# Chunked attention followed by a squared-ReLU feed-forward layer on one core: block 0 worked by halves of the heads, and a new order of block 2's loads

## The chip, the cores and the metric

The kernel runs on one core of one Trainium2 chip. Its time is the device time of one launch in microseconds (us). The time before is the median of 3 runs; beside it stands one execution that the hardware profiler recorded.

## The reference: what is computed

```python
q_c, k_c, v_c = (t.reshape(B, H, nc, 64, D) for t in (q, k, v))       # B, H, S, D = 8, 8, 576, 64
attn = softmax(q_c @ k_c.transpose(0, 1, 2, 4, 3) / sqrt(D))          # each chunk of 64 tokens by itself
x    = (attn @ v_c).transpose(0, 2, 1, 3).reshape(B * S, H * D)       # 4608 tokens x 512
h    = maximum(x @ w_in, 0)                                           # w_in 512 x 2048
out  = h * h @ w_out                                                  # w_out 2048 x 512, float32
```

All inputs and the output are float32 in DRAM. The kernel computes in bfloat16 and accumulates in float32.

## The kernel before, in words

**Groups and blocks.** The 4608 tokens are 18 groups of 256 tokens (four chunks of 64); two groups are a block of 512 tokens, so there are nine blocks. For a group the kernel loads q, k and v, transposes q and k so that the head dimension lies on the partitions, multiplies chunk by chunk into scores (`scores`, matmuls in L483), takes the exponential on ScalarE (L494), and multiplies with v (`values`, L510). V has a column of ones beside each head, so the last column of a product is the sum of a row of weights; VectorE takes its reciprocal (L442) and multiplies (L443) into x. Transposed x (`xT`) goes into the feed-forward layer. Its first half (`ffn_in`, L579) computes, for each of 16 tiles `ft` of 128 features, four matmuls over `dt`, the four slices of 128 of the 512 columns of x. Heads 0 and 1 make slice 0, heads 6 and 7 make slice 3. ScalarE applies ReLU out of PSUM (L590), VectorE or ScalarE squares (L598, L596). The second half multiplies with `w_out` (`ffn_out_by_ft`, L901, in block 0; `ffn_out` with sums of sub-matrices, L780, in the later blocks; from block 4 on the first half, too, is built from sums of sub-matrices, L657).

**The order of the work.** It is written out by hand: each engine executes its instructions in the order in which the program emits them. The start (L967 to L1002) is straight code; after it each block has a table of slots, one per feature tile or group of matmuls, which says what is emitted behind which slot (`at(slot, f, ...)`, L1004 to L1077). Attention of a later block is thus laid between the feed-forward matmuls of an earlier one.

**The start before.** SP's queue gets the loads of q and k for groups 0 and 1 (all eight heads, 256 tokens each), then V in nine pieces, then `w_in` by slices of 256 columns (`load_w_in`: all 512 rows, so the first slice carries feature tiles 0 and 1), then `w_out`. q and k of each group arrive as rows of two neighbouring tokens (512 bytes for each head). TensorE transposes q0, k0, q1 (`transpose_paired`, L400), makes the scores of group 0, transposes k1, and goes on through scores, values and the transposes of x (`transpose_x_early`, L521). Between these, `keep_busy(n)` (L433) issues n matmuls of 128 columns whose results nobody reads: 8, 6, 10, 4 and 8. The first feed-forward matmul comes after the last transpose of x. Tiles 0 and 1 are done in two halves of 256 tokens, since the second half of xT is copied last. GpSimd casts the weights to bfloat16 in slices (L334, L342); ScalarE casts one half of the first slice (L333).

**Buffers.** The PSUM pool `ps_ffn` has four banks, taken in turn; two double banks `ps_att` and `ps_att2` serve attention in turn. Staged weights go through five buffers `w_st`; q and k through five buffers `qk_st`. V lies in five tiles `ve_sb` (even heads) and eleven tiles `vo_sb` (odd heads, whose chunks are shifted by 64 tokens). The loads of SP's queue share eight completion semaphores in turn, so from the ninth on a load is issued when the one eight before it has landed.

**Blocks 1 and 2.** From group 4 on, q and k are not transposed by TensorE: GpSimd casts them (`C`, L449 and L454) and SP issues a transposing DMA (`TD`, L460). While block 0 runs, SP issues the loads of block 2 (groups 4 and 5): q and k of both, then V of group 4, then V of group 5. While block 1 runs, SP issues the two transposing DMAs (slots 21 and 25), then the loads of q and k of groups 6 and 7. The scores of groups 4 and 5 come at slots 36 and 37 of block 1, their values at 38 and 40.

## Time and profile before

| | before |
|---|---|
| time, median of 3 runs | 278.54 us (277.97 to 279.36) |
| time of the profiled execution | 276.91 us |
| its span, first to last instruction | 275.1 us |
| granted TensorE clock | 1.000 |
| TensorE (PE), busy share of the span | 96% |
| VectorE (DVE) | 72% |
| ScalarE (ACT) | 61% |
| GpSimd (POOL) | 33% |

The profiled execution's own time is 1.8 us longer than its span: that much lies before its first and after its last instruction. Times within the trace count from the first instruction. A row of a timeline gives the start, the length, engine, line, operation, names (out<-in), the count, and in brackets the idle time of the engine just before with what ended it. PE's matmuls overlap, so the length of a group has the last one's way through the array in it. For SP's queue (SPq) a row is the issue of a DMA, not its transfer; its length holds what the issue had to wait for.

### The profile page before, as it was taken

The page shows a single profiled execution, that of the slowest core. Times are in us where ns is not written, and L with a number is a line of the kernel's source. Part 1 is how long each engine was busy: PE and PEld are TensorE (multiplying, and loading weights), DVE is VectorE, ACT ScalarE, POOL GpSimd, SP SyncE. Part 2 cuts the span into 40 slices and gives each one's busy share as a digit, 9 for nine tenths or more (in the row PEclk, how much of TensorE's full clock was granted, in tenths as well). Part 3 has the DMA queues.
Part 4 walks back from the last instruction along what each step waited for, and adds up shares of the span by engine and source line. Part 5 has one row for each costly group of instructions (what it writes and reads, how often), then busy time and mean ns, then how long its engine had stood idle before and what let it go on. Part 6 is the DMA issues. An engine that isn't in the chain of part 4 may idle for free.

```text
span 275.1 us, 7923 instructions
## 1 busy us (share of the span) xinstructions
PE 264.9 (96%) x3261; PEld 203.4 (74%) x3261; DVE 199.2 (72%) x365; ACT 168.3 (61%) x300; POOL 89.6 (33%) x122
## 2 busy tenths in 40 slices
PE   2999999999999999999999999999999999999995
PEld 2764445888774588447878888888888888888884
DVE  1457514999538592499989998799779877994752
ACT  1657614894458883877678765565746665756430
POOL 2048834240360012040245224551643212331600
PEclk9999999999999999999999999999999999999999
DMA  7999999999999999999999999697999530220223
GB/s 216 262 352 389 361 332 270 339 213 172 262 210 218 238 234 218 275 223 178 228 236 197 218 238 194 103 220 196 244 187 224 123 76 2 99 55 7 71 83 114
DMA packets 136056, 55.60 MB, mean 202 GB/s; under 512 B 104273, under 2 KB 131921, under 8 KB 136017
## 3 DMA queue, kind: packets, MB, share of 16 engines
q1 hardware_dynamic: 133248, 46.54, 74.0%
q0 software_dynamic: 2624, 8.39, 9.6%
q8 instruction: 26, 0.43, 0.6%
q10 hardware_dynamic: 144, 0.13, 0.1%
q14 instruction: 14, 0.11, 0.1%
HBM read 36.70 MB, written 9.44 MB: 168 GB/s over the span
## 4 chain that ended last, share of the span: by engine, by line
PE 87%; DMA 4%; SPq 3%; DVE 3%; ACT 1%; issue 1%; ACTq 0%; DVEq 0%
PE ps_ffn L657 22%; PE ps_out L780 22%; PE ps_ffn L579 17%; PE ps_ffn L780 14%; PE ps_ffn L901 5%; PE ps_att L510 3%; PE ps_att L540 2%; DMA vo_sb<-in_v_dram 2%; PE ps_att L483 2%; DMA xT<-x 2%; DVE gT L598 2%; SPq L266 1%; SPq L308 1%; SPq L312 1%; DVE x L443 1%; ACT e L494 1%
## 5 line engine op out<-in xcount | busy, mean ns | idle before, releaser
L579 PE MATMUL ps_ffn<-xT,w_in_bf 128*128 128x512 bf16 (+1 forms) x328 | 57.8, 333 | 0.0
L780 PEld LDWEIGHTS <-w_st 128*128 128x128 bf16 x512 | 48.9, 98 | 6.6 <-DVE w_st L614 0.5
L665 DVE CUSTOM_DVE_ANT_0 relu<-ps_ffn,w_st 128x512 f32<-128x512 f32 x60 | 39.3, 684 | 13.0 <-PE ps_ffn L657 11.6
L579 PEld LDWEIGHTS <-w_in_bf 128*128 128x128 bf16 x328 | 31.2, 98 | 21.6 <-POOL w_in_bf L334 0.2
L598 DVE TENSOR_TENSOR gT<-relu 128x256 bf16<-128x256 bf16 (+2 forms) x68 | 34.1, 537 | 17.8 <-ACT relu L590 17.3
L590 ACT ACTIVATE relu<-ps_ffn 128x256 bf16<-128x256 f32 (+2 forms) x82 | 39.4, 501 | 9.4 <-PE ps_ffn L579 8.6
L657 PE MATMUL ps_ffn<-qk_st,w_in_bf 128*128 128x256 bf16 x240 | 35.3, 273 | 0.1
L657 PEld LDWEIGHTS <-w_in_bf 128*128 128x128 bf16 x320 | 30.7, 98 | 4.1 <-issue 0.3
L809 POOL DMA_DIRECT2D out_dram<-o_sb x24 | 17.6, 733 | 43.6 <-DVE o_sb L614 23.3
L780 PEld LDWEIGHTS <-gT 128*128 128x128 bf16 x296 | 28.6, 98 | 3.3
L780 PE MATMUL ps_out<-w_out_bf,w_st 128*128 128x256 bf16 x240 | 30.8, 273 | 0.0
L699 ACT ACTIVATE w_st<-ps_ffn 128x512 f32<-128x512 f32 x20 | 11.9, 597 | 29.6 <-PE ps_ffn L657 29.6
L443 DVE TENSOR_TENSOR x<-ps_att,recs 128x512 bf16<-128x512 f32 x36 | 24.9, 692 | 1.2
L657 PEld LDWEIGHTS <-qk_st 128*128 128x128 bf16 x240 | 22.6, 98 | 3.2 <-DVE qk_st L614 0.3
L657 PE MATMUL ps_ffn<-xT,qk_st 128*128 128x256 bf16 x160 | 23.9, 273 | 0.0
L676 POOL TENSOR_TENSOR qk_st<-relu 128x512 bf16<-128x512 f32 x10 | 10.3, 1034 | 41.6 <-DVE relu L665 38.1
L494 ACT ACTIVATE e<-ps_att 128x1024 bf16<-128x1024 f32 x18 | 18.3, 1025 | 8.5 <-PE ps_att L483 8.5
L676 POOL TENSOR_TENSOR gT<-relu 128x512 bf16<-128x512 f32 x10 | 10.3, 1033 | 35.4 <-DVE relu L665 30.5
L449 POOL CAST qkb<-qk_st 128x1024 bf16<-128x1024 f32 x12 | 13.0, 1082 | 14.9 <-DMA qk_st<-in_q_dram 14.9
L674 ACT ACTIVATE gT<-relu 128x512 bf16<-128x512 f32 x28 | 17.7, 631 | 0.0
L780 PE MATMUL ps_ffn<-w_out_bf,w_st 128*128 128x256 bf16 x144 | 17.7, 273 | 0.0
L614 DVE TENSOR_TENSOR w_st<-gT,w_st 128x1024 bf16<-128x1024 bf16 x26 | 16.8, 682 | 0.0
(92 smaller groups left out, 428.7 us busy)
## 6 DMA issues: line engine op xcount, KB each, us to landing
qk_st<-in_q_dram SPq DMA_DIRECT2D x16, 512.0 KB, 5.6
out_dram<-o_sb POOLq DMA_DIRECT2D x28, 256.0 KB, 3.9
qk_st<-in_k_dram SPq DMA_DIRECT2D x24, 256.0 KB, 5.6
ve_sb<-in_v_dram SPq DMA_DIRECT2D x32, 128.0 KB, 3.9
w_st<-in_moe_w_in_dram SPq DMA_DIRECT2D x8, 512.0 KB, 5.9
w_st<-in_moe_w_out_dram SPq DMA_DIRECT2D x8, 512.0 KB, 5.5
vo_sb<-in_v_dram SPq DMA_DIRECT2D x24, 128.0 KB, 3.6
qk_st<-in_k_dram SPq DMA_DIRECT2D x4, 512.0 KB, 5.8
```

Source lines behind the costliest of these rows:

```text
L443: nc.vector.tensor_tensor(out=x, in0=o[:, :, :, 0:D], in1=rec.to_broadcast([128, 2, n, D]), op=ALU.mult)
L494: nc.scalar.activation(out=e_out, in_=s_in, func=AF.Exp, scale=scale)
L579: nc.tensor.matmul(out=h[:, 0:n], lhsT=w_in_bf[:, dt, ft * 128:(ft + 1) * 128], rhs=xT[:, c // 128:(c + n) // 128, dt, :], start=(dt == 0) ...
L590: nc.scalar.activation(out=rl[:, 0:n], in_=h[:, 0:n], func=AF.Relu)
L598: nc.vector.tensor_tensor(out=dst, in0=src, in1=src, op=ALU.mult)
L614: nc.vector.tensor_tensor(out=out, in0=in0, in1=in1, op=op)
L657: nc.tensor.matmul(out=bank[:, f * GT:(f + 1) * GT], lhsT=a[:, dt, ft * 128:(ft + 1) * 128], rhs=b[:, :, dt, :], start=(first and f == 0 a ...
L665: nc.vector._custom_dve(TENSOR_ADD_SAT, out=out, in0=in0, in1=in1, s0=BIG, s1=0.0)
L674: engine.activation(out=dst, in_=r, func=AF.Square)
L676: engine.tensor_tensor(out=dst, in0=r, in1=r, op=ALU.mult)
L780: nc.tensor.matmul(out=out_ps, lhsT=lhsT, rhs=b[:, i, :], start=(first and i == 0 and (last or t == 0)), stop=(i == HF - 1), skip_group_ch ...
L809: dma.dma_start(out=out[t0:t0 + GT, col:col + HD].rearrange("(t p) d -> p t d", p=128), in_=o_sb.rearrange("p (t d) -> p t d", d=HD))
```

## The change

Three things change at the start, and one in blocks 1 and 2.

**Halves.** Block 0 is split by heads, not by tokens. Half 0 is heads 0 to 3 of all 512 tokens, half 1 heads 4 to 7. q and k arrive as rows of four neighbouring tokens (1,024 bytes for each head). V of a half is six loads: for each pair of heads the even head (four tiles of 128 tokens) and the inner three tiles of the odd head, and two half tiles at the edges. A half has the same count and shapes of transposes (32), scores matmuls (32), exponentials (one of 128x1024), values matmuls (two times 16), reciprocals and multiplies as a group had. The copies of transposed k are shared: one by ScalarE, one by VectorE; those of q stay on VectorE.

**Loads.** SP's order becomes q, k, V of half 0; q, k of half 1; rows 0 to 255 of the first 512 columns of `w_in` (in two loads); V of half 1; rows 256 to 511 of the same columns (in two loads); then `w_in` from slice 2 on as before. GpSimd casts all of it; ScalarE's cast is gone.

**TensorE's order.** Since half 0 yields slices 0 and 1 of x, the feed-forward tiles 0 to 3 start before half 1 is done: their matmuls for dt 0 and 1 stand behind the scores of half 1 and around its values, those for dt 2 behind the transposes of x, then those for dt 3 with ReLU and square. The four tiles hold the four banks of `ps_ffn` meanwhile. All 64 matmuls of block 0's first half have 512 columns (before, 16 of 72 had 256). Of the `keep_busy` matmuls 16 of 36 stay: 8 before the scores of half 0 and 8 behind them. The square of tile 3 in block 0 goes to VectorE.

**Block 2.** While block 0 runs, SP gets q and k of groups 4 and 5 and V of group 4 alone. In block 1 the casts and transposing DMAs of groups 4 and 5 are emitted at slots 16 and 20, and V of group 5 at slot 21, behind both transposing DMAs.

```diff
+    v_first = w_pool.tile([128, 4, n_hp, D + 1], FP32, name="ve_first")
+    v_mid = w_pool.tile([128, 3, n_hp, D + 1], FP32, name="vo_mid")
...
-            if i == 0 and c:
-                return lambda: nc.scalar.copy(out=w_in_bf[:, :, c:c + n], in_=st[:, :, c:c + n])
...
+    def load_w_in_half(r):
+        st = w_st[next(n_staged) % 5].rearrange("p (a f) -> p a f", a=2)
+        for c in (0, 256):
+            nc.sync.dma_start(
+                out=st[:, :, c:c + 256],
+                in_=moe_w_in[256 * r:256 * r + 256, c:c + 256].rearrange("(a p) f -> p a f", p=128))
+            nc.gpsimd.tensor_copy(
+                out=w_in_bf[:, 2 * r:2 * r + 2, c:c + 256], in_=st[:, :, c:c + 256])
...
+        for hp in range(NH):
+            copy = nc.vector.tensor_copy if hp or not which else nc.scalar.copy
+            copy(out=qkT[:, which, hp].rearrange("c (p i) -> c p i", i=4),
+                 in_=psb[:, hp].rearrange("c i p -> c p i"))
...
+    def first_tile(ft, dts):
+        if dts[0] == 0:
+            first_h.append(ps_ffn.tile([128, 512], FP32, name="ps_ffn"))
+        for dt in dts:
+            nc.tensor.matmul(
+                out=first_h[ft],
+                lhsT=w_in_bf[:, dt, ft * 128:(ft + 1) * 128],
+                rhs=xTs[0][:, :, dt, :],
+                start=(dt == 0), stop=(dt == n_dt - 1), skip_group_check=True)
+
+    def first_in():
+        for ft in range(4):
+            first_tile(ft, (3,))
+            squared(0, ft, first_h[ft], 0, BT, ft)
+            yield
+        yield from ffn_in(0, [(0, BT, range(4, n_ft))])
...
+    for half in range(2):
+        qk_half, v_half = half_loads(half)
+        go(qk_half)
+        if half:
+            load_w_in_half(0)
+        go(v_half)
+    load_w_in_half(1)
+    transpose_half(0, 0, ffn_bank())
+    transpose_half(0, 1, ffn_bank())
     keep_busy(8)
...
+    scores_half(0)
     keep_busy(8)
...
+    values_half(0, 0)
+    values_half(0, 1)
+    transpose_half(1, 0, ffn_bank())
+    transpose_x_half(0, 0, ffn_bank(), act)
+    transpose_half(1, 1, ffn_bank())
+    transpose_x_half(0, 1, ffn_bank(), act)
+    scores_half(1)
+    first_tile(0, (0, 1))
+    first_tile(1, (0, 1))
+    values_half(1, 0)
+    first_tile(2, (0, 1))
+    values_half(1, 1)
+    first_tile(3, (0, 1))
+    transpose_x_half(1, 0, att_bank()[:, 0:256], act)
+    transpose_x_half(1, 1, att_bank()[:, 0:256], nc.vector.tensor_copy)
+    for ft in range(4):
+        first_tile(ft, (2,))
+    first_ffn_in = first_in()
...
-            loads, go_slots = pieces(far), range(17)
+            loads, go_slots = itertools.chain(*map(qk_pieces, far), v_pieces(far[0])), range(17)
...
-                for slot, f in ((16 + 4 * i, C), (21 + 4 * i, TD), (36 + i, SC), (38 + 2 * i, AV),
+                for slot, f in ((16 + 4 * i, C), (16 + 4 * i, TD), (36 + i, SC), (38 + 2 * i, AV),
                                 (41 + 2 * i, XT)):
                     at(slot, f, g)
+            at(21, lambda: go(v_pieces(nxt[1])))
```

More of the change, by code (lines that the diff above doesn't have):

```diff
@@ L239 @@
     n_rec = itertools.count()
-    v_even = [w_pool.tile([128, 2, n_hp, D + 1], FP32, name=f"ve_sb{i}") for i in range(NV)]
-    v_odd = [w_pool.tile([128, n_hp, D + 1], FP32, name=f"vo_sb{i}") for i in range(NO)]
+    v_first = w_pool.tile([128, 4, n_hp, D + 1], FP32, name="ve_first")
+    v_mid = w_pool.tile([128, 3, n_hp, D + 1], FP32, name="vo_mid")
+    v_even = [v_first[:, 2 * i:2 * i + 2] for i in range(2)] + [
+        w_pool.tile([128, 2, n_hp, D + 1], FP32, name=f"ve_sb{i}") for i in range(2, NV)]
+    v_odd = [v_mid[:, i - 1] if 0 < i < 4 else w_pool.tile(
+        [128, n_hp, D + 1], FP32, name=f"vo_sb{i}") for i in range(NO)]
     for vt in v_even:
@@ L314, in v_pieces @@
                 in_=v[b, 1::2, s:s + m, :].rearrange("h s d -> s h d")))
-        if g < 2:
-            yield from [even[0], *odd[:-1], even[1], odd[-1]]
-        else:
-            yield from even + odd
+        yield from even + odd
     def go(pieces):
@@ L515, in values, with half_loads, rows, even @@
             out_of_x(x[:, t].rearrange("p h a d -> p a h d"), ps, n_hp)
-    def transpose_x_early(g, t):
-        psb = ps_ffn.tile([128, 512], FP32, name="ps_ffn").bitcast(BF16)
-        x = state["x", g]
-        for hp in range(n_hp):
+    NH, HH = 2, H // 2
+    def half_loads(half):
+        b, s0 = chunks[0][0]
+        hs = slice(HH * half, HH * half + HH)
+        def rows(which, src):
+            return lambda: nc.sync.dma_start(
+                out=loaded(half, which).rearrange("p (h e) -> p h e", h=HH),
+                in_=src[b, hs, s0:s0 + BT, :].rearrange("h (s i) d -> s h (i d)", i=4))
+        hps = slice(NH * half, NH * half + NH)
+        def even(hp):
+            return lambda: nc.sync.dma_start(
+                out=v_first[:, :, NH * half + hp, 0:D],
+                in_=v[b, HH * half + 2 * hp, s0:s0 + BT, :].rearrange("(t p) d -> p t d", p=128))
+        def odd(hp):
+            return lambda: nc.sync.dma_start(
+                out=v_mid[:, :, NH * half + hp, 0:D],
+                in_=v[b, HH * half + 2 * hp + 1, s0 + CH:s0 + BT - CH, :].rearrange(
+                    "(t p) d -> p t d", p=128))
+        def edge(n):
+            p = CH if n == 0 else 0
+            s = s0 + 128 * n - CH + p
+            return lambda: nc.sync.dma_start(
+                out=v_odd[n][p:p + CH, hps, 0:D],
+                in_=v[b, HH * half + 1:HH * half + HH:2, s:s + CH, :].rearrange("h s d -> s h d"))
+        return [rows(0, q), rows(1, k)], [even(0), odd(0), edge(0), edge(4), even(1), odd(1)]
@@ new lines, in load_w_in_half, with transpose_half @@
+    def load_w_in_half(r):
[6 more added lines that the diff above has]
+                out=w_in_bf[:, 2 * r:2 * r + 2, c:c + 256], in_=st[:, :, c:c + 256])
+    def transpose_half(half, which, bank):
+        if ("half", half) not in state:
+            state["half", half] = qkT_tile().rearrange("c w t h q -> c w (t h q)").rearrange(
+                "c w (h s) -> c w h s", h=NH)
+        qkT = state["half", half]
+        psb = bank.bitcast(BF16)[:, 0:1024].rearrange("c (h i q) -> c h i q", h=NH, i=4)
+        src = loaded(half, which).bitcast(BF16).rearrange("p (h i d) -> p h i d", h=HH, i=4)
+        for hp in range(NH):
+            for i in range(4):
+                for a in range(2):
+                    nc.tensor.transpose(
+                        out=psb[64 * a:64 * a + 64, hp, i, :],
+                        in_=src[:, 2 * hp + a, i, 1::2],
+                        identity=ident)
+        for hp in range(NH):
+            copy = nc.vector.tensor_copy if hp or not which else nc.scalar.copy
+            copy(out=qkT[:, which, hp].rearrange("c (p i) -> c p i", i=4),
+                 in_=psb[:, hp].rearrange("c i p -> c p i"))
@@ new lines, in scores_half @@
+    def scores_half(half):
+        qkT = state["half", half]
+        ps = att_bank()
+        for hp in range(NH):
+            for t in range(4):
+                for a in range(2):
+                    for p in range(2):
+                        c = p ^ a
+                        o0 = a * 512 + hp * 256 + t * 64
+                        cols = slice((2 * t + p) * CH, (2 * t + p + 1) * CH)
+                        nc.tensor.matmul(
+                            out=ps[64 * c:64 * c + 64, o0:o0 + 64],
+                            lhsT=qkT[64 * a:64 * a + 64, 1, hp, cols],
+                            rhs=qkT[64 * a:64 * a + 64, 0, hp, cols],
+                            start=True, stop=True)
+        e = e_tile()
+        state["e half", half] = e.rearrange("p (a h t q) -> p a h t q", a=2, h=NH, t=4)
+        nc.scalar.activation(out=e, in_=ps, func=AF.Exp, scale=scale)
@@ new lines, in values_half @@
+    def values_half(half, hp, n_fill=0):
+        e = state["e half", half]
+        if hp == 0:
+            state["x half", half] = att_pool.tile(
+                [128, 2, n_hp, 2, D], BF16, name="x", bufs=3).rearrange(
+                    "p t h a d -> p (t h a d)").rearrange("p (h t a d) -> p h t a d", h=NH, t=4, a=2)
+        x = state["x half", half]
+        ps = att_bank().rearrange("p (a f) -> p a f", a=2)
+        fill(n_fill, ps[:, 0, 384:512])
+        for t in range(4):
+            for a in range(2):
+                for p in range(2):
+                    c = p ^ a
+                    vb = (v_odd[t + p] if a else v_even[t // 2][:, t % 2]).bitcast(BF16)
+                    nc.tensor.matmul(
+                        out=ps[64 * p:64 * p + 64, a, t * (D + 1):t * (D + 1) + D + 1],
+                        lhsT=e[64 * c:64 * c + 64, a, hp, t, :],
+                        rhs=vb[64 * c:64 * c + 64, NH * half + hp, 1::2],
+                        start=True, stop=True)
+        out_of_x(x[:, hp].rearrange("p t a d -> p a t d"), ps, 4)
@@ L521, in transpose_x_early, with transpose_x_half @@
+    def transpose_x_half(half, hp, bank, copy):
+        psb = bank.bitcast(BF16)[:, 0:512]
+        x = state["x half", half]
+        for t in range(4):
             nc.tensor.transpose(
-                out=psb[:, hp * 128:(hp + 1) * 128],
-                in_=x[:, t, hp].rearrange("p a d -> p (a d)"),
+                out=psb[:, t * 128:t * 128 + 128],
+                in_=x[:, hp, t].rearrange("p a d -> p (a d)"),
                 identity=ident)
-        copy = nc.vector.tensor_copy if t and g else nc.scalar.copy
@@ L526, in transpose_x_early, with fill @@
-        copy(
-            out=x_tile(g // 2)[:, g % 2 * 2 + t].rearrange("p h q -> p (h q)"),
-            in_=psb[:, 0:512])
+        copy(out=x_tile(0)[:, :, NH * half + hp, :], in_=psb.rearrange("p (t q) -> p t q", t=4))
+    def fill(n, out):
+        for _ in range(n):
+            nc.tensor.matmul(out=out, lhsT=ident, rhs=ident, start=True, stop=True)
     def transpose_x(g):
@@ L571, with squared @@
     FT_ORDER = [*range(n_ft // 2, n_ft), *range(n_ft // 2)]
+    def squared(j, u, h, c, n, ft):
+        gT = gT_main.rearrange("p (u h) (f t) -> p u h f t", u=2, f=4)
+        if n == 512 or u % 2 == 0:
+            state["rl"] = state.get("rl", -1) + 1
+            rl_tile = relu_sb[state["rl"] % 4]
+            if j < 3:
+                rl_tile = rl_tile.bitcast(BF16)
+            state["rl tile"] = rl_tile
+        rl_tile = state["rl tile"]
+        rl = rl_tile[:, u % 2 * 512:] if n < 512 else rl_tile
+        nc.scalar.activation(out=rl[:, 0:n], in_=h[:, 0:n], func=AF.Relu)
+        u0, u1 = c // GT, (c + n) // GT
+        dst = gT[:, u0:u1, ft // 4, ft % 4, :]
+        src = rl[:, 0:n].rearrange("p (u t) -> p u t", t=GT)
+        if (n == 512 and ft in SQUARES_ON_ACT and (j or ft > 3)) or (n < 512 and ft in (12, 3)):
+            nc.scalar.activation(out=dst, in_=src, func=AF.Square)
+        else:
+            nc.vector.tensor_tensor(out=dst, in0=src, in1=src, op=ALU.mult)
     def ffn_in(j, parts):
-        gT = gT_main.rearrange("p (u h) (f t) -> p u h f t", u=2, f=4)
         xT = xTs[j]
@@ L583, in ffn_in @@
                     start=(dt == 0), stop=(dt == n_dt - 1))
-            if n == 512 or u % 2 == 0:
-                state["rl"] = state.get("rl", -1) + 1
-                rl_tile = relu_sb[state["rl"] % 4]
-                if j < 3:
-                    rl_tile = rl_tile.bitcast(BF16)
-            rl = rl_tile[:, u % 2 * 512:] if n < 512 else rl_tile
-            nc.scalar.activation(out=rl[:, 0:n], in_=h[:, 0:n], func=AF.Relu)
-            u0, u1 = c // GT, (c + n) // GT
-            dst = gT[:, u0:u1, ft // 4, ft % 4, :]
-            src = rl[:, 0:n].rearrange("p (u t) -> p u t", t=GT)
-            if (n == 512 and ft in SQUARES_ON_ACT) or (
-                    n < 512 and ft in (12, 3)) or (j == 0 and u == 0):
-                nc.scalar.activation(out=dst, in_=src, func=AF.Square)
-            else:
-                nc.vector.tensor_tensor(out=dst, in0=src, in1=src, op=ALU.mult)
-            yield
+            squared(j, u, h, c, n, ft)
+            yield
+    first_h = []
+    def first_tile(ft, dts):
+        if dts[0] == 0:
+            first_h.append(ps_ffn.tile([128, 512], FP32, name="ps_ffn"))
+        for dt in dts:
+            nc.tensor.matmul(
+                out=first_h[ft],
[8 more added lines that the diff above has]
+        yield from ffn_in(0, [(0, BT, range(4, n_ft))])
     a11, a12 = w_in_bf[:, 0:2, 0:d_ff // 2], w_in_bf[:, 2:4, 0:d_ff // 2]
@@ L965, in AV1, with ffn_bank @@
         values(g, [1])
-    HT = BT // 2
-    go(pieces([0, 1]))
-    cast_first = load_w_in(0, n_cast=2)
-    TE(0)
-    transpose_qk(1, ps_ffn, None)
-    SC(0)
-    transpose_qk(1, None, ps_ffn)
-    keep_busy(8)
-    AV(0, [0])
-    SC(1)
-    keep_busy(6)
-    AV(0, [1])
-    transpose_x_early(0, 0)
-    keep_busy(10)
-    transpose_x_early(0, 1)
-    AV(1, [0])
-    AV(1, [1])
-    keep_busy(4)
-    transpose_x_early(1, 0)
-    cast_first()
-    keep_busy(8)
-    transpose_x_early(1, 1)
-    first_ffn_in = ffn_in(0, [(0, HT, (0, 1)), (HT, HT, (0, 1)), (0, BT, range(2, n_ft))])
-    next(first_ffn_in)
-    next(first_ffn_in)
-    for i in range(1, 8):
+    def ffn_bank():
+        return ps_ffn.tile([128, 512], FP32, name="ps_ffn")
+    act = nc.scalar.copy
+    for half in range(2):
[7 more added lines that the diff above has]
+    transpose_half(0, 1, ffn_bank())
+    keep_busy(8)
+    scores_half(0)
+    keep_busy(8)
+    values_half(0, 0)
[16 more added lines that the diff above has]
+    first_ffn_in = first_in()
+    for i in range(2, 8):
         load_w_in(i, n_cast=2 if i < 5 else 1)
```

## The prediction, made before the changed kernel ran

> **What bounds the kernel now.** I read the page first, its busy shares and its summary of the chain that ended last.

> ```profile
> PE 264.9 (96%) x3261; PEld 203.4 (74%) x3261; DVE 199.2 (72%) x365; ACT 168.3 (61%) x300; POOL 89.6 (33%) x122
> ...
> PE 87%; DMA 4%; SPq 3%; DVE 3%; ACT 1%; issue 1%; ACTq 0%; DVEq 0%
> ```

> TensorE is busy for 96% of the span and holds 87% of the chain. Its waits by engine, asked from 17.4 to 275 us, have one row:

> ```profile
> PE ps_ffn L657 <- DVE qk_st L614: 0.2, 1, 0.2
> ```

> So behind the start the time is the sum of TensorE's work; an edit pays by what it takes off that work or by how much earlier the full stream begins. The chain of the first 80 us says what holds the start:

> ```profile
> 10.73 4.93 DMA vo_sb<-in_v_dram
> ...
> 17.46 14.01 PE ps_ffn L579 x72
> 31.47 7.77 PE ps_ffn L901 x36
> ```

> The last of the V loads lands at 15.66, then come values, x and its transposes; at 17.46 the feed-forward layer starts, and its first half ends at 31.47. Until 17.46 TensorE does no feed-forward work. That is the stage in which to count.

> **The change, part by part.** *Feed-forward matmuls.* The groups of L579 from 17.46 to 31.3 us:

> ```profile
> L579 PE MATMUL ps_ffn<-xT,w_in_bf 128*128 128x512 bf16 x56 | 12.2, 379 | 0.0
> L579 PE MATMUL ps_ffn<-xT,w_in_bf 128*128 128x256 bf16 x16 | 1.9, 273 | 0.0
> ```

> 12.2 / 56 = 0.218 us each, and 1.9 us for sixteen of half the width, about as much as eight wide ones: that rewrite is free. Eight of the 64 (tiles 0 to 3, slices 0 and 1) move ahead of the last transposes of x, into time when TensorE waits: 8 x 0.218 = 1.74 us. What counts against it is how late the other 56 start, which the chain of half 1 decides.

> *The loads.* Three windows (the last figure is GB/s):

> ```profile
> 3.00:8.00 5.00, 2.38 (x38) 1.90 (x40) 1.29 (x2) 0.63 (x2) 0.00 (x0) 1.00 1.15 347
> 9.40:12.90 3.50, 3.31 (x86) 2.70 (x90) 1.64 (x4) 2.75 (x4) 0.00 (x0) 1.00 1.38 223
> 17.46:24.00 6.54, 6.54 (x39) 3.77 (x40) 3.81 (x7) 5.09 (x12) 5.18 (x9) 1.00 1.08 373
> ```

> q and k in pieces of 512 bytes move at 347, V in pieces of 256 bytes at 223, weights in pieces of 1,024 bytes at 373. q and k now come in pieces of 1,024 bytes: 0.524 MB takes 1.41 instead of 1.51 us. I take 0.1 off each of the four; the bounds are 0 and twice that. [...]

> TensorE's first groups:

> ```profile
> 4.77 1.06 PE L400 MATMUL ps_ffn<-ident,qk_st 128*64 128x128 bf16 x16 [4.77 <-DMA qk_st<-in_q_dram]
> 6.26 1.06 PE L400 MATMUL ps_ffn<-ident,qk_st 128*64 128x128 bf16 x16 [0.42 <-DMA qk_st<-in_k_dram]
> 7.75 1.06 PE L400 MATMUL ps_ffn<-ident,qk_st 128*64 128x128 bf16 x16 [0.43 <-DMA qk_st<-in_q_dram]
> 8.74 0.64 PE L483 MATMUL ps_att<-qkT 64*64 64x64 bf16 x32
> ```

> k of group 0 lands at 6.25; k of half 0 then at 6.05. V of half 0 follows, 0.524 MB at 223 GB/s, 2.35 us: 8.4. Then q and k of half 1 at 9.8 and 11.2, the first weights at 12.6, V of half 1 about 15.0.

> *Chain of half 0.* The rows that carry it, of VectorE, of ScalarE and of TensorE:

> ```profile
> 5.88 1.29 DVE L409 COPY qkT<-ps_ffn 128x512 bf16<-128x512 bf16 x2 [5.88 <-PE ps_ffn L400]
> ...
> 13.23 0.21 DVE L442 RECIPROCAL recs<-ps_att 128x8 f32<-128x8 f32 x1 [0.46 <-PE ps_att L510]
> ...
> 15.20 0.21 DVE L442 RECIPROCAL recs<-ps_att 128x8 f32<-128x8 f32 x1 [1.03 <-PE ps_att L510]
> ...
> 16.30 0.69 DVE L443 TENSOR_TENSOR x<-ps_att,recs 128x512 bf16<-128x512 f32 x1
> ```
> ```profile
> 9.44 1.02 ACT L494 ACTIVATE e<-ps_att 128x1024 bf16<-128x1024 f32 x1 [1.00 <-PE ps_att L483]
> ...
> 13.52 0.58 ACT L526 COPY xT<-ps_ffn 128x512 bf16<-128x512 bf16 x1 [0.26 <-PE ps_ffn L521]
> ```
> ```profile
> 12.83 0.22 PE L510 MATMUL ps_att<-ve_sb,e 64*64 64x65 bf16 x2 [0.19 <-DVE x L443]
> ...
> 13.09 0.40 PE L521 MATMUL ps_ffn<-ident,x 128*128 128x128 bf16 x4
> ```

> The k transposes end at 6.05 + 1.06 = 7.1. Eight idle matmuls follow (1.03 below, 0.9 without the last one's tail) and cover the copies of k, which now run on two engines at once. Scores at 8.0; the exponential begins 0.70 behind them (8.74 to 9.44) and takes 1.02: 9.7. V is there since 8.4. Values begin at 9.8, VectorE 0.4 to 0.5 behind (12.83 to 13.23, more at the slow pace told below), and two reciprocals with their multiplies take 1.79 (15.20 to 16.99): x of half 0 at 12.1.

> *Chain of half 1.* VectorE has three copies queued behind these multiplies, 3 x 0.645 = 1.94: 14.0. This is the wait that the change adds: q and k of half 1 have landed by 11.2, but the scores need the copies, and the early feed-forward tiles stand behind the scores on TensorE. The last half of the scores costs 0.2, the exponential begins at 14.45 and ends at 15.5. Meanwhile TensorE does four early matmuls (0.87). Values at 15.55, VectorE 0.40 behind, x of the first pair after half of the 1.79, at 16.9, of the second at 17.74; then 0.43 from transposes to ScalarE's copy (13.09 to 13.52) and 0.58: 17.95. So the 56 begin at 18.0, 0.54 later than the stream before. The second pair's copy ends at about 18.6, before its first reader at 18.9.

> *Sum.* 1.74 won, 0.54 lost by the later start, and 0.2 lost because the four first tiles finish 0.22 apart while ScalarE needs about 0.58 for an evacuation of this size, so the fifth tile's bank comes late once (bounds 0 and 0.4). That makes 1.0 us. The dropped idle matmuls filled waits and are worth nothing by themselves.

> *What comes after.* Does the rest arrive 1.0 earlier too? Three loads with little room:

> ```profile
> 41.69 1.04 POOL L342 CAST w_out_bf<-w_st 128x1024 bf16<-128x1024 f32 x1 [0.91 <-DMA w_st<-in_moe_w_out_dram]
> ```
> ```profile
> 43.25 1.90 PE L901 MATMUL ps_ffn<-w_out_bf,gT 128*128 128x512 bf16 x8
> ```
> ```profile
> 61.66 6.17 SPq L460 DMA_TRANSPOSE qkT<-qkb  x2
> DMA to landing us min/median/max: 4.9/4.9/4.9
> 70.22 0.37 PE ps_att L483 x32
> ...
> 74.00 0.39 PE ps_att L510 x27
> ```

> The last `w_out` cast ends at 42.73; its first reader is the third of the eight matmuls, at 43.7: 1.0 of room, plus the 0.4 that the four shorter q, k loads give all later ones. Of the two transposing DMAs the second, issued at 64.8, lands 4.9 later (the middle row is that DMA alone), at 69.7, and its scores stand at 70.2: 0.5 of room, not enough. That is what moving V of group 5 mends: its 0.46 MB, 2.1 us at 223 GB/s, now go behind both. V of group 5 in turn waits for two issues of 3 us, lands near 70, and its values stand at 74.0. SP's further order is the same. So I let the 1.0 pass whole: 276.91 - 1.0 = 275.9 for a profiled execution. The median of the runs lies 1.63 above that execution, so **277.5 us**, 0.37% less. About 0.5% (1.4 us) is what a measurement here can tell from no change.

> **The rivals.**

> *A sooner chain, gain 1.9.* TensorE has two paces, as eight idle matmuls show early and late:

> ```profile
> 10.36 1.03 PE L433 MATMUL ps_ffn<-ident 128*128 128x128 bf16 x8
> ...
> 16.43 0.61 PE L433 MATMUL ps_ffn<-ident 128*128 128x128 bf16 x8
> ```

> The granted clock is 1.00 in every window, so this pace shows in lengths alone. If the fast one comes before the scores of half 0, idle matmuls and k transposes lose about 0.4 each; that, and no late bank, makes 1.0 + 0.9. For it: TensorE works from 6.05 on nearly without pause. Against: it did so before from 7.75, and was slow still at 10.36. 276.6.

> *A slow TensorE at the early tiles, slower by 1.9.* From 10.4 to 14.0 TensorE has transposes and nothing else, with waits between. If it is at the slow pace there, 128 columns cost (1.03 - 0.61) / 8 = 0.052 more, a matmul of 512 columns 0.21 more. Four early ones delay x's transposes by 0.84 and the two others by 0.4; the next eight cost 1.7 before the pace returns: 2.9 in all, less 1.0, 1.9 slower: 280.4. It decides if the pace is not fast at 14.0. Against: from 6.05 to 10.4 there is more unbroken work than before from 7.75 to 10.36. [...]

> *A load arrives late, gain 0.3.* Before, V of both groups landed from about 9.25 (q of group 1 at 7.75, its k one load of 1.5 later) to 15.66, 6.4 us, where 1.05 MB at 223 GB/s is 4.7. If all of those 1.7 fall on V of half 1, it lands at 16.7 for values at 15.55 and 16.2; and eight loads in flight hold fewer bytes when two of them are of 32 KB. The first pair's pieces come first, so 0.7 is lost: 278.2.

> *The early tiles are not early.* If VectorE's copies end so late that the eight matmuls only push the values back, the 0.54 remains alone: 279.1.

> **How the numbers follow.** Forecast 0.40 (0.12 of it beyond 0.5% faster), the sooner chain 0.25 (0.23 faster), a late load 0.17 (nearly all within 0.5%), the slow TensorE 0.15 (0.12 slower), no early tiles 0.03. Faster 0.35, same 0.52, slower 0.13. The range reaches from beyond the sooner chain, 276.0, to inside the slow TensorE, 279.9; the forecast's own range, with both ends of loads and banks, is 276.9 to 278.3.

> **What would show it.** Right: the first of the 56 (dt 2 of tile 0) near 18.0, the last before `w_out`'s near 30.4, four early ones under the exponential of half 1, its scores behind VectorE's third copy near 14.0, no new waits of TensorE after 19 us, the second transposing DMA landed before 68.5. Wrong: early matmuls 0.43 apart, values of half 1 released by a DMA, or waits on casts near 25 and 42 us.

## The result and the profile after

| | before | after |
|---|---|---|
| median of 6 runs, same chip | 278.25 us (277.29 to 279.36) | 282.52 us (280.42 to 285.45) |
| profiled execution | 276.91 us, span 275.1 | 281.96 us, span 280.2 |

The ratio is 1.0163, with a 95% interval of 1.0130 to 1.0196: 1.6% slower, where 0.4% faster was forecast and 279.9 us was the upper end of the range. Here and below the medians are over all executions and the ratios over the fast ones alone, since single executions run in a slower state (one of the kernel with wider loads took 452 us).

The two lines of the page of after that answer to the first ones shown of before, the busy engines and the chain that ended last:

```profile
PE 266.4 (95%) x3233; PEld 202.1 (72%) x3233; DVE 202.2 (72%) x367; ACT 165.3 (59%) x293; POOL 90.8 (32%) x123
...
PE 81%; DMA 8%; DVE 4%; ACT 3%; SPq 1%; issue 1%; POOL 0%; ACTq 0%; POOLq 0%
```

28 matmuls are gone (3261 to 3233: 20 idle ones and 8 by joining halves), and TensorE is still busy for 1.5 us longer; the other 3.6 us of the longer span are waits. TensorE's waits in after, from 17.4 us to the end (line, releaser, us in total, times, longest):

```profile
PE ps_ffn L781 <- issue: 2.1, 1, 2.1
PE ps_att L642 <- DVE x L442: 0.8, 1, 0.8
PE ps_att L482 <- DMA qkT<-qkb: 0.6, 1, 0.6
PE ps_att L622 <- DVE x L442: 0.4, 1, 0.4
PE ps_ffn L781 <- DVE qk_st L738: 0.2, 1, 0.2
PE ps_att L509 <- DMA vo_sb<-in_v_dram: 0.2, 1, 0.2
```

Before had the fifth of these alone (there L657 and L614). Held against the same matmuls of before, after runs 0.95 us late at the first matmul with `w_out` (32.25 against 31.30), 1.6 at the scores of group 7 (91 us), 2.3 at 125 us, 2.7 just ahead of 252 us and 4.9 from 254 us on. The largest single step, 2.15 us, has no releaser. The chain of after at that place, then that of before (start, length, what):

```profile
250.46 0.87 PE ps_out L904 x8
251.34 0.92 PE ps_ffn L781 x7
252.26 2.15 issue
254.41 0.28 PE ps_ffn L781
```
```profile
247.80 0.87 PE ps_out L780 x8
248.67 0.06 issue
248.73 1.05 PE ps_ffn L657 x8
249.78 0.87 PE ps_out L780 x8
```

At 248.73 of before and 251.34 of after stands a branch, between the same matmuls (in before a short "issue" of 0.06 marks it): there the program decides, by a flag, between its rest (which is what runs here) and a repeat with maxima (L1313 of after, L1179 of before, `tc.If(again > 0)`). In after TensorE goes on for seven matmuls behind it and then stands still for 2.15 us, and the profile shows nothing that it waits for. The change touches nothing there.

The start, in TensorE's timeline of after:

```profile
12.25 1.06 PE L569 MATMUL ps_ffn<-ident,qk_st 128*64 128x128 bf16 x16
...
14.00 0.43 PE L588 MATMUL ps_att<-qkT 64*64 64x64 bf16 x16
...
15.08 1.89 PE L713 MATMUL ps_ffn<-xT,w_in_bf 128*128 128x512 bf16 x4
...
17.27 1.01 PE L713 MATMUL ps_ffn<-xT,w_in_bf 128*128 128x512 bf16 x2
...
18.46 0.60 PE L713 MATMUL ps_ffn<-xT,w_in_bf 128*128 128x512 bf16 x2
...
19.96 1.89 PE L713 MATMUL ps_ffn<-xT,w_in_bf 128*128 128x512 bf16 x8
21.89 0.38 PE L699 MATMUL ps_ffn<-xT,w_in_bf 128*128 128x512 bf16 x1
```

The first four early matmuls take 1.89 us, the last eight of the same shape also 1.89: TensorE was at its slow pace until about 18.3. And slice 2 of `w_in` was not there sooner than that either. GpSimd's row of its cast (released by the load), and the windows 13 to 17 us of after and of before:

```profile
21.16 1.17 POOL L333 CAST w_in_bf<-w_st 128x512 bf16<-128x512 f32 x2 [2.56 <-DMA w_st<-in_moe_w_in_dram]
```
```profile
13.00:17.00 4.00, 3.56 (x54) 1.54 (x54) 1.30 (x3) 2.14 (x3) 1.04 (x2) 1.00 0.82 197
```
```profile
13.00:17.00 4.00, 3.43 (x82) 2.57 (x72) 2.62 (x6) 1.81 (x4) 0.21 (x1) 1.00 1.09 318
```

Half of that cast is 0.6 us, so tile 4, which needs it, could start at 21.8 at the soonest. In these 4 us the DMA engines moved 197 GB/s where they had moved 318, and their share fell from 1.09 to 0.82. That too few bytes were under way is a reading so far; the runs with wider loads test it.

### The profile page after: what moved, and what is told of

Same layout as the page of the kernel before. It is cut to its first block, busy times and chain, and to the rows that moved or that the text cites. A ratio compares the mean times of both kernels' runs of the same rounds, so it can differ in the third digit from the quotient of the medians.

```text
span 280.2 us, 7871 instructions
## 1 busy us (share of the span) xinstructions
PE 266.4 (95%) x3233; PEld 202.1 (72%) x3233; DVE 202.2 (72%) x367; ACT 165.3 (59%) x293; POOL 90.8 (32%) x123
## 3 DMA queue, kind: packets, MB, share of 16 engines
HBM read 36.70 MB, written 9.44 MB: 165 GB/s over the span
## 4 chain that ended last, share of the span: by engine, by line
PE 81%; DMA 8%; DVE 4%; ACT 3%; SPq 1%; issue 1%; POOL 0%; ACTq 0%; POOLq 0%
PE ps_ffn L781 21%; PE ps_out L904 21%; PE ps_ffn L699 12%; PE ps_ffn L904 11%; PE ps_ffn L1025 5%; DMA qk_st<-in_k_dram 3%; DMA qkT<-qkb 3%; PE ps_att L509 2%; DVE gT L692 2%; PE ps_ffn L713 2%; PE ps_att L482 2%; PE ps_att L642 1%; ACT e L493 1%; DMA vo_sb<-in_v_dram 1%; PE ps_ffn L569 1%
## 5 line engine op out<-in xcount | busy, mean ns | idle before, releaser
L699 PE MATMUL ps_ffn<-xT,w_in_bf 128*128 128x512 bf16 (+1 forms) x304 | 54.4, 335 | 0.0
L692 DVE TENSOR_TENSOR gT<-relu 128x512 bf16<-128x512 bf16 (+2 forms) x68 | 35.2, 558 | 16.2 <-ACT relu L685 15.8
L685 ACT ACTIVATE relu<-ps_ffn 128x512 bf16<-128x512 f32 (+2 forms) x80 | 39.0, 512 | 10.6 <-PE ps_ffn L699 7.9
L699 PEld LDWEIGHTS <-w_in_bf 128*128 128x128 bf16 x304 | 28.9, 98 | 20.8 <-POOL w_in_bf L333 0.5
L781 PEld LDWEIGHTS <-w_in_bf 128*128 128x128 bf16 x320 | 30.7, 98 | 4.0 <-issue 0.3
L442 DVE TENSOR_TENSOR x<-ps_att,recs 128x512 bf16<-128x512 f32 x36 | 24.9, 691 | 1.2
L493 ACT ACTIVATE e<-ps_att 128x1024 bf16<-128x1024 f32 x16 | 16.3, 1026 | 7.0 <-PE ps_att L482 7.0
L798 ACT ACTIVATE gT<-relu 128x512 bf16<-128x512 f32 x28 | 17.7, 632 | 0.0
L904 PE MATMUL ps_ffn<-w_out_bf,w_st 128*128 128x256 bf16 x144 | 17.7, 273 | 0.0
```

The costliest lines, as they stand in the source:

```text
L442: nc.vector.tensor_tensor(out=x, in0=o[:, :, :, 0:D], in1=rec.to_broadcast([128, 2, n, D]), op=ALU.mult)
L493: nc.scalar.activation(out=e_out, in_=s_in, func=AF.Exp, scale=scale)
L685: nc.scalar.activation(out=rl[:, 0:n], in_=h[:, 0:n], func=AF.Relu)
L692: nc.vector.tensor_tensor(out=dst, in0=src, in1=src, op=ALU.mult)
L699: nc.tensor.matmul(out=h[:, 0:n], lhsT=w_in_bf[:, dt, ft * 128:(ft + 1) * 128], rhs=xT[:, c // 128:(c + n) // 128, dt, :], start=(dt == 0) ...
L781: nc.tensor.matmul(out=bank[:, f * GT:(f + 1) * GT], lhsT=a[:, dt, ft * 128:(ft + 1) * 128], rhs=b[:, :, dt, :], start=(first and f == 0 a ...
```

## The experiments

Three explanations stood against each other: (a) the stall behind the branch comes from the length of TensorE's program, which is 56 rows shorter (28 matmuls and their 28 weight loads; the traces have 6,522 rows before and 6,466 after); (b) the slow pace and the late loads at the start, whose delay is carried to the end; (c) block 2's new order of loads. All medians are in us; the kernel before ran beside each, between 277.5 and 278.1.

| kernel | median | ratio to before (95%) | stall behind the branch in the trace |
|---|---|---|---|
| after + 28 small matmuls | 277.51 | 0.9993 (0.9968 to 1.0019) | none |
| after + 28 idle matmuls at the start | 278.22 | 1.0013 (0.9985 to 1.0041) | none |
| after, wider loads | 281.27 | 1.0125 (1.0063 to 1.0187) | 2.25 |
| after, wider loads + 28 idle matmuls | 277.81 | 0.9993 (0.9956 to 1.0030) | none |
| before, 54 rows fewer | 281.93 | 1.0128 (1.0083 to 1.0173) | 2.34 |
| before, 54 fewer + 54 rows | 278.78 | 1.0039 (1.0008 to 1.0070) | none |
| after + 128 small matmuls (256 rows) | 282.58 | 1.0162 (1.0083 to 1.0242) | 1.97 |
| after + 4 small matmuls (8 rows) | 279.24 | 1.0031 (0.9998 to 1.0064) | 0.39 |
| after + 14 small matmuls (28 rows) | 278.29 | 1.0024 (0.9995 to 1.0054) | none |
| after, block 2's old order | 283.52 | 1.0168 (1.0114 to 1.0222) | 2.01 |
| before, block 2's new order | 277.54 | 1.0009 (0.9975 to 1.0044) | none |
| after once more | 282.22 | 1.0181 (1.0121 to 1.0241) | 2.15 |
| wider loads + 28 small | 277.55 | 0.9977 (0.9953 to 1.0001) | none |
| the same, block 2's old order | 277.40 | 0.9967 (0.9937 to 0.9996) | none |

**Rows alone.** 28 matmuls of one row and one column, at the start, where TensorE waits for its first data anyway:

```diff
+    ps = ps_ffn.tile([128, 512], FP32, name="ps_ffn")
+    for _ in range(28):
+        nc.tensor.matmul(out=ps[0:1, 0:1], lhsT=ident[:, 0:1], rhs=ident[:, 0:1], start=True, stop=True)
     act = nc.scalar.copy
     for half in range(2):
```

> The changed kernel with 28 matmuls of one row and one column ahead of the first transposes: TensorE's program is as long as before the change (56 instructions more), with next to no work. Theory 'fetch': the gap of 2.15 us near 254 is gone and the time is about 2 us shorter, with the start unchanged (second half of block 0 near 32.2, early matmuls 0.43 apart). Rival (chance or timing): the gap stays, the time stays near 282.5.

277.51: the whole loss is gone. These matmuls cost 0.84 us of idle time and leave the pace at 12 us slow (sixteen transposes at 12.13 still take 1.06). In this trace the pace turns fast sooner than in after (the four early matmuls at 14.85 take 1.04), so this run alone does not rule the pace out. The second trace of the unchanged kernel, below, does: it has the fast pace from about 12 us on, and the stall and the loss all the same.

**The kernel before with fewer rows.** No work is moved; its 36 idle matmuls are issued as 9 of four times the width:

```diff
+    busy = [0]
...
-        for _ in range(n):
-            nc.tensor.matmul(out=ps[:, 0:128], lhsT=ident, rhs=ident, start=True, stop=True)
+        was, busy[0] = busy[0], busy[0] + n
+        for _ in range(busy[0] // 4 - was // 4):
+            nc.tensor.matmul(out=ps, lhsT=ident, rhs=ident[:, 0:4].to_broadcast([128, 4, 128]), start=True, stop=True)
```

> The kernel before, with its idle matmuls written as a quarter as many of four times the width: the same idle work, but 54 rows fewer in TensorE's program, so that the branch to the last part stands at row 6054 instead of 6108 (6052 in the changed kernel, where TensorE stood still for 2.15 us just behind it). Theory 'rows' (the stall at the branch comes from the length of TensorE's program and from nothing that the change does to the work): a stall of 2.1 us appears in L657 near 250 us, six matmuls behind the branch, and the time is 2.1 to 4 us above before, 279.7 to 281.5. Rival 'order' (the loss comes from the new order of the work): no stall, 277.6 within 0.6, since nothing of the work is moved.

281.93, somewhat over the 281.5 that was the forecast's end: nearly the same loss, without a line of the change. Its chain at the branch:

```profile
250.20 0.87 PE ps_out L783 x8
251.07 0.70 PE ps_ffn L660 x5
251.77 2.34 issue
254.11 0.50 PE ps_ffn L660 x3
```

The stall comes after five matmuls; by rows it should have been six. The control gives it its 54 rows back as 27 small matmuls ahead of the first transposes:

> The kernel before with its idle matmuls as a quarter as many of four times the width, as in the run with fewer rows, and with 27 matmuls of one row and one column ahead of the first transposes: TensorE's program has again the rows of before, the branch stands at 6108. Theory 'place': no stall, no wait for the transposing DMAs near 69 us, 277.5 to 278.6. Rival (the wide idle matmuls themselves cost time): 279.5 or more, without a stall.

278.78, no stall; the remaining 0.4% (0.1 to 0.7) is left to the wide idle matmuls at the start. The rival of this run falls.

**Length or place?** 128 small matmuls in after, 72 at the start and 28 behind each group of idle ones, make its program longer than that of before:

> The changed kernel with 128 matmuls of one row and one column added (72 at the start, 28 behind each group of eight idle matmuls), 256 rows of TensorE's program in all: the branch to the last part stands at row 6308 = 6052 + 256. Theory 'place' (the stall comes where a packet of 256 rows ends just behind the branch): the stall of 2 us is back, 7 matmuls behind the branch, and the time with it, 281 to 284, the added work included, which may cost up to 1 us. Rival 'length' (a shorter program than some threshold stalls): no stall, 277.5 to 279.

282.58. The chain shows the stall back at the same place, seven matmuls behind the branch:

```profile
251.04 0.91 PE ps_ffn L783 x7
251.95 1.97 issue
253.92 0.28 PE ps_ffn L783
```

So it is not a short program that stalls; the stall comes back with 256 rows more. The page of after says what has that size, in its table of DMA queues (packets, MB, share of 16 engines):

```profile
q8 instruction: 26, 0.43, 0.6%
```

0.43 MB in 26 packets are 16 KB each, and 6,466 rows in 26 packets about 250 rows each; the run with 256 rows more has 27 packets. So I read queue 8 as the one that brings TensorE's instructions. Asked by windows, it begins no packet in after from 237 to 251.9 us. For 251.9 to 254.4 us the view shows (GB/s in 40 slices of 0.06 us, then the queues):

```profile
GB/s 262 262 131 131 0 0 0 0 0 0 0 0 0 0 0 0 0 0 0 0 0 0 0 0 0 0 0 0 0 0 0 0 0 0 0 0 0 0 0 0
...
q14 instruction: 4, 0.03, 4.7%
q8 instruction: 1, 0.02, 2.5%
```

All five packets begin by 252.15, just ahead of the stall (252.26); the one of queue 8 takes 1.0 us (2.5% of 16 engines' 2.5 us). No other begins until TensorE goes on at 254.41. Before has the same five packets behind its branch (window 249 to 252 us) and no stall. The difference lies ahead of the branch. In all nine traces without a stall a packet of queue 8 moves 3.4 to 5.1 us ahead of the branch, by its start; in the six with a stall of about 2 us the last one moves 14.9 to 15.3 us ahead of it, and TensorE goes on 2.2 to 2.5 us after the packet that follows the branch. As these traces read, TensorE works on behind the branch where a packet moved those 3.4 to 5.1 us ahead of it, and waits for the packet behind the branch where none did.

Two runs move the branch by small steps, with 4 and with 14 small matmuls:

> The changed kernel with 4 matmuls of one row and one column at the start instead of none: TensorE's program is 8 rows longer, the branch to the last part stands at row 6060 instead of 6052. In the changed kernel the stall came 7 matmuls (14 rows) behind the branch, in the kernel before with fewer rows (branch at 6054) 5 or 6 matmuls behind it. Theory 'rows' with a fixed place in the program (about row 6073) at which TensorE's next instructions are not there: the stall of 2 us stays and comes 3 matmuls behind the branch, 281 to 283. Rival 'clock' (what helped in the kernel with 28 such matmuls was their work at the start): half of the gain at most, no shift of the stall. Rival 'distance' (the stall always follows the branch by a fixed time): 7 matmuls behind the branch.

> The changed kernel with 14 matmuls of one row and one column at the start: TensorE's program is 28 rows longer, the branch stands at row 6080, past the place of the stall (about row 6073). Theory 'rows' with a fixed place: no stall, 277.2 to 278.5, as with 28 of them. Rival 'distance': a stall of 2 us stays, 281 to 283. Rival 'clock': half of the gain.

With 8 rows more the stall comes three matmuls behind the branch instead of seven, four matmuls or 8 rows sooner, as forecast; but it is 0.39 long, not 2, and the median is 279.24:

```profile
249.81 0.35 PE ps_ffn L781 x3
250.17 0.39 issue
250.55 0.72 PE ps_ffn L781 x5
```

In that trace a packet of queue 8 moves at 247.6, 2.2 us ahead of the branch, which after lacks, and TensorE goes on 3.0 us after it. Why one moved ahead of the branch there stays open. With 28 rows more the branch lies behind the place, and there is no stall (278.29).

**Block 2.** Its old order in after, and its new order in before:

```diff
-            loads, go_slots = itertools.chain(*map(qk_pieces, far), v_pieces(far[0])), range(17)
+            loads, go_slots = pieces(far), range(17)
...
-                for slot, f in ((16 + 4 * i, C), (16 + 4 * i, TD), (36 + i, SC), (38 + 2 * i, AV),
+                for slot, f in ((16 + 4 * i, C), (21 + 4 * i, TD), (36 + i, SC), (38 + 2 * i, AV),
...
-            at(21, lambda: go(v_pieces(nxt[1])))
```

> The changed kernel with block 2's loads and transposing DMAs in the order of before; block 0 as changed, TensorE's program as short as the changed one's. Theory 'rows': the stall of 2.1 us behind the branch stays, and at most the 0.6 us goes that the scores of group 7 waited for their transposing DMA at 91 us: 281.5 to 282.5. Rival 'block 2' (the new order of block 2's loads costs most of the loss): back near before, 277.6 to 279.

> The kernel before with block 2's new order of loads alone (V of its first group, both transposes, V of its second group), its TensorE program as long as before. Theory 'rows': no stall at the branch; the transposes of groups 4 and 5 go out some 2 us sooner, nothing waits for them, and the later transposes of groups 6 and 7 are late by less than 0.7 us: 277.6 to 278.4. Rival 'block 2': over 279.5.

> The changed kernel with the wider loads and the 28 small matmuls (no stall, loads on time), and block 2's loads in the order of before. Theory: with the loads on time the transposing DMAs of groups 4 and 5 land ahead of their scores in either order, so block 2's order is worth nothing: within 0.5 us of the same kernel with the new order, 277.3 to 277.9. Rival (the new order is what keeps TensorE from a wait at 69 us): a wait of 0.5 us or more for a transposing DMA near 69 us, 278 or more.

283.52, 277.54 and 277.40: the order of block 2 carries none of the loss. The old order had a price of its own in after, a wait for group 4's transposing DMA at 70 us (TensorE's waits from 66 to 72 us):

```profile
PE ps_att L482 <- DMA qkT<-qkb: 2.1, 1, 2.1
```

This wait was not forecast (281.5 to 282.5). So the new order did what it is built for: in after those scores wait for nothing. It may have given 0.6 back at 91 us, where the transposing DMA of group 7 landed at 91.4 instead of 87.7. With the wider loads and the rows restored the two orders are equal within their intervals. The trace of the last run shows neither wait, but it can't tell: TensorE itself is late there (first matmul with `w_out` at 32.85), and the second transposing DMA lands 0.04 us ahead of its scores.

**The start.** 28 idle matmuls of full size ahead of the first transposes (`keep_busy(28)`); wider loads (V's edges of both halves in one load of all odd heads, each half of the first `w_in` columns in one load of 512 columns: 16 loads ahead of slice 2 instead of 20); both; and the wider loads with the small matmuls:

```diff
...
-        return [rows(0, q), rows(1, k)], [even(0), odd(0), edge(0), edge(4), even(1), odd(1)]
+        return [rows(0, q), rows(1, k)], [even(0), odd(0), *([] if half else [edge(0), edge(4)]), even(1), odd(1)]
...
+        nc.sync.dma_start(
+            out=st, in_=moe_w_in[256 * r:256 * r + 256, 0:512].rearrange("(a p) f -> p a f", p=128))
         for c in (0, 256):
-            nc.sync.dma_start(
-                out=st[:, :, c:c + 256],
-                in_=moe_w_in[256 * r:256 * r + 256, c:c + 256].rearrange("(a p) f -> p a f", p=128))
```

> The changed kernel with 28 idle matmuls of 128 columns ahead of the first transposes, where TensorE waits for q (from about 1.7 to 4.7 us). Theory 'pace': TensorE's slow pace up to 18.3 us delays the feed-forward stream; then the early matmuls stand 0.22 apart instead of 0.43, x of half 1 is done near 17.7 and the second half of block 0 starts near 30.5 instead of 32.25. Rival 'loads': the slice of w_in for tile 4 lands at 21.1 and is cast by 21.8 whatever the pace; then TensorE stalls before tile 4 and the second half of block 0 still starts at 32.1 to 32.3. Both at once: the pace changes, the time does not. Besides, TensorE's program has the length it had before the change again: theory 'fetch' (the 2.15 us gap near 254 comes from where the branch falls in the instruction stream) expects no such gap and about 2 us less in all; its rival (chance, or the length of the start) expects the gap again.

> The changed kernel with 16 instead of 20 loads ahead of slice 2 of w_in: each half's 512 columns of w_in in one load, the edges of odd V for all heads in two loads. Theory 'loads': with eight loads in flight the small ones starve the DMA engines between 13 and 17 us (197 GB/s against 318 before); now slice 2 lands 1 to 1.5 us sooner, near 19.8, and the second half of block 0 starts up to 1 us sooner if the pace lets it. Theory 'pace' alone expects slice 2 sooner and the start of the second half unchanged at 32.2, since the slow matmuls end at 21.85 anyway. The gap near 254 stays at about 2 us (TensorE's program is unchanged).

> Both edits together. If slow pace and late loads each alone hold tile 4 at 21.9, only this one starts it near 19.8: second half of block 0 near 30.2 to 30.6, 1.7 to 2 us sooner than the changed kernel and about 1 sooner than before; without the gap near 254 the whole is 276.5 to 278, even with or below the kernel before. If only one of the two counted, this equals that one's run.

> The changed kernel with three edits: V's odd heads of a half come in one load of twice the size where there were two, the slices of w_in come in one DMA of 512 columns instead of two of 256 (fewer loads ahead of slice 2), and 28 matmuls of one row and one column stand at the start, only so that TensorE's program has the length of before. Theory 'rows' with the late loads as the second term: the second half of block 0 begins 0.5 to 0.9 us sooner than before, no stall at the branch, 276.7 to 277.1. Rival (the gain of block 0 is lost again behind it whatever the loads do): 277.6.

The 28 idle matmuls take back the loss, but they also restore the rows, so this run tells nothing of the pace by itself. Nor did its trace show the early matmuls 0.22 us apart, as theory 'pace' forecast: the granted clock was 0.62 from 13 to 17 us, and the four took 1.89. The wider loads alone leave the stall and most of the loss, though slice 2 lands at 18.9 instead of 21.1. With the rows restored as well (the expectation speaks of V's odd heads in one load; the edit joins V's edges), the start may win something: tile 4 begins at 20.49 and the first matmul with `w_out` at 30.85, 0.45 sooner than before. The ratio is 0.23% below before, with an interval that ends at no change; its twin with block 2's old order is 0.33% below (0.04 to 0.63%). These two have the lowest ratios of the study, but 277.55 misses the forecast of 276.7 to 277.1 and lies at its rival's 277.6: how much of the gain of block 0 reaches the end is not shown. The window from 13 to 17 us of the first of them:

```profile
13.00:17.00 4.00, 3.29 (x78) 1.58 (x74) 1.71 (x4) 2.14 (x3) 1.17 (x2) 1.00 1.06 296
```

The DMA engines moved 296 GB/s, half as much again as in after. Over the traces of the changed kernel and its variants this window has 166 to 254 GB/s in the eight with 20 loads ahead of slice 2 and 292 to 319 in the four with 16.

**What a stall drags behind it.** The windows of after with wider loads, around its stall (us, busy times of the five engines, granted clock, DMA share, GB/s):

```profile
248.00:250.00 2.00, 0.73 (x7) 0.40 (x5) 0.00 (x0) 1.11 (x2) 0.00 (x0) 1.00 0.09 25
250.00:252.00 2.00, 1.02 (x6) 0.73 (x7) 0.49 (x1) 0.00 (x0) 0.00 (x0) 0.76 0.00 0
252.00:254.00 2.00, 2.00 (x11) 1.45 (x10) 0.20 (x1) 0.58 (x1) 1.03 (x1) 0.50 0.03 8
254.00:256.00 2.00, 2.00 (x18) 1.71 (x17) 1.92 (x3) 0.00 (x0) 0.00 (x0) 0.88 0.00 0
```

Behind the 2.25 us of standstill the granted clock falls to 0.50, and the matmuls up to 256 us take 1.7 us longer than behind the stall of after. In the first trace of after, and in its second, the clock stayed at 1.00; but the mean clock of five of its first six runs is 0.994, and 0.006 of 280 us is 1.7 us. By this estimate the stall costs about 2.2 us in some executions and nearly 4 in others. The fall is not bound to the branch: it also follows a wait of 2.08 us for a DMA at 70 us (after with block 2's old order, 0.69 from 72 to 76 us) and one of 2.14 at 92 us (28 idle matmuls, 0.57 from 92 to 96 us).

**After once more.** A second trace of the unchanged changed kernel:

> The changed kernel once more, unchanged, for a second trace: which of its five losses come in every execution and which by chance. Theory: the stall of 2.1 us behind the branch and a late third slice of w_in come again; the start of TensorE's fast pace (18.3 us in the first trace, 10.4 to 14 us in the others) and the waits at 91 and 125 us move. 281 to 283.

```profile
PE ps_ffn L781 <- issue: 2.1, 1, 2.1
PE ps_ffn L713 <- POOL w_in_bf L556: 1.4, 1, 1.4
PE ps_att L482 <- DMA qkT<-qkb: 1.3, 2, 0.7
PE ps_ffn L781 <- DVE qk_st L738: 0.7, 1, 0.7
```

The stall is the same to 0.01 us and so is its place. The pace is not: the four early matmuls take 1.04 here, and the first of the 56 starts at 18.25 instead of 19.96. That gain is lost at once to a cast of slice 1 (1.4), whose load landed at 19.55; the first matmul with `w_out` starts at 32.14, as late as in the first trace. The wait on VectorE near 125 us (0.8 in the first trace) is gone.

## Why the prediction was wrong, point by point

**The step that failed.** "The dropped idle matmuls filled waits and are worth nothing by themselves", and with it "that rewrite is free". As work they were worth nothing. As 56 rows of TensorE's program they kept the branch at 249 us where TensorE works on behind it. Without them TensorE stands still 14 rows behind the branch: 2.15 us, and in part of the executions, by the estimate from the mean clock of 0.994, up to 1.7 more. Adding the rows back took the loss away, taking them from before made it, and 256 rows more brought it back. None of the rivals held this, so the range did not either. In the traces the wait is 2.0 to 2.3 us long and comes 10 to 14 rows behind the branch, not at it, and only where the last packet of queue 8 moved 14.9 to 15.3 us ahead of the branch. That rows without work could have such a price, I had not weighed.

**The chain of the halves** was right where TensorE had its fast pace. k of half 0 landed at 6.05, as forecast. The first of the 56 matmuls was forecast for 18.0; over the nine traces that keep this order and have no full-size idle matmuls ahead of the first transposes (the run with 128 small matmuls left out) it stands at 18.03 to 18.60 seven times, and at 19.96 and 20.57 in the two whose pace turned fast only near 18 us or later. So the rival of the slow TensorE was no rival for every execution but a case of some, and costs 1.4 to 2.5 us at that place. The moment at which the pace turns fast varies over these traces from about 10 us (after with block 2's old order) to 18.3, and between two executions of the unchanged after from about 12 to 18.3. The prediction weighed it by how unbroken TensorE's work is; that this decides it, no run here shows.

**The late bank** (0.2) did not show: 0.04 us lie between the eighth matmul and tile 4 where the weights are there.

**The loads** were the second term that was mis-sized. The rival "a load arrives late" named what the runs with wider loads speak for, fewer bytes in eight loads under way (197 GB/s from 13 to 17 us in after, 296 with wider loads), but looked for it at V of half 1 (price 0.7). The loads that came late are those behind it, slices 1 and 2 of `w_in`. Over the six traces that have the change's loads and at most 28 small matmuls, the first matmul with `w_out` stands at 30.59 to 32.25, mean 31.45, where before has 31.30: the forecast 1.0 is lost there, with the stall or without it. With 16 loads instead of 20 it stands at 30.75 to 30.85 in three traces and at 32.85 in the one whose pace turned late: of the 1.0 about half is real.

**"So I let the 1.0 pass whole."** There was little to pass. But the argument on block 2 had its second transposing DMA land before 68.5, and it landed at 69.4, still soon enough. Late loads are not the whole reason: in the kernel before with the new order alone it landed at 69.6, where before has 69.7, so moving V of group 5 behind it brought 0.1 us there and not 2.1; with the wider loads and the new order it landed at 66.4 to 69.0. What I did not look at is what moves behind it: V of group 5 now stands on the queue ahead of group 7's transpose, which landed 3.7 us later than before, and the room at 91 us is gone. The order alone does not explain that: this DMA landed 2.3 us later in the kernel before with the new order, but 2.2 later in after with the old order, and 4.1 later in before with 54 rows fewer.

**What stays open.** The stall is not the whole loss. In the seven executions with it whose clock stayed at 1.00 the time is 280.4 to 282.3, on average 3.4 us over the kernel before run beside them, of which the stall is about 2.2. In the traces the rest lies ahead of the branch, which after reaches 2.6 us later than before, and before with 54 rows fewer 2.3 later; with the wider loads it comes 0.9 us sooner. Group 7's transposing DMA lands at 91.4 to 91.8 in four of the six traces with the stall (88.3 and 89.9 in the others) and at 87.7 to 90.1 in the others but one (92.0, the 28 idle matmuls). Whether such delays are bound to the rows or are chance, these traces do not settle. Nor is it settled what decides whether the next packet moves ahead of the branch.

## What to carry to other kernels

An instruction that costs no time can still have a price by its place, as the rows here had: when an edit adds or drops instructions on the engine that bounds a kernel, look at each branch behind the edit for an "issue" gap without releaser, and move the branch by some 30 rows before judging the edit (28 removed the stall here, 8 left 0.39 us of it). Where such a gap is there, judge the edit by a pair of kernels with equal rows: here the change is 1.6% slower as written and, with 28 small matmuls for equal rows, between 0.3% faster and 0.2% slower. And count loads, not only bytes, where a fixed number may be under way, eight here: four loads fewer ahead of the first bottleneck brought the second half of block 0 forward by about half a microsecond in three of four traces.
